# Batch 0 of an FFT filter ahead of an MLP: real and imaginary spectrum rows side by side, frequencies k1 and k1 + 12 on the two partition halves

## The chip, the core and the metric

The kernel runs on one core of a Trainium2 chip. The metric is the device time of one launch in microseconds. An engine's name stands for its instruction stream: PE is TensorE (PEld its weight loads), DVE is VectorE, ACT is ScalarE, POOL is GpSimd, SP is SyncE. POOL and SP also issue DMAs.

## What is computed

The input x has 8 batches of 3008 positions and 256 channels. Along the positions each channel is filtered in the frequency domain, with a complex filter for each frequency and channel; then every position goes through a two-layer MLP with an exact GELU, 256 to 2048 to 256.

```python
X = np.fft.rfft(x, axis=1)                      # x: (8, 3008, 256)
Y = X * (filt_r + 1j * filt_i)[None, :, :]      # filters: (1505, 256)
y = np.fft.irfft(Y, n=3008, axis=1)
h = y.reshape(24064, 256) @ w_in                # (256, 2048)
g = 0.5 * h * (1.0 + erf(h / np.sqrt(2.0)))
out = g @ w_out                                 # (2048, 256)
```

## The kernel before

**The transform.** 3008 is 47 x 64 (NA, NB), and the transform is done in two steps by matmuls with tables of sines: over the 47 (first index k1, of which 24 are needed, K1) and over the 64. Batch 0 has a path of its own, whose stages are c1, c1t, c2, c3, c3t and c4; it is the only work until its end, apart from tables and loads. Batches 1 to 7 go through s1, s2, s3, s4, in small pieces put between the matmuls of the MLP.

**Batch 0, stage by stage.** `c1` multiplies x by the 47-point table T1c and evicts into y_sb. `c1t(q)` transposes four k1 at a time into b_sb, with an eviction by ACT (the first by DVE and ACT together). `c2(p)` multiplies two k1 (2p and 2p + 1) by the table T2 into one PSUM bank: real and imaginary rows of one k1 lie on 128 partitions, and the two k1 stand side by side. DVE then multiplies that bank by the filter tile F, once by the real and once by the imaginary part of the filter (the tile p, 128 x 1024). `c3(p)` multiplies the result back with T3, and with T3i, a copy of T3 with real and imaginary rows exchanged and signs turned; the results go to vt_sb. `c3t` and `c4` transpose and do the inverse 47-point step into the ring y_sb, which the MLP reads.

**The filters.** F has 128 partitions. Rows 0 to 63 take the filter from HBM (32 rows directly, 32 in mirrored order), and rows 64 to 127 are a copy of rows 0 to 63, made by `dup_filters`: the first four k1 by DVE, the other twenty by POOL. `load_filters` is called for 4, 8 and 12 k1, and makes four DMAs each time. `move_filters` (SP) takes the filters from F to Fu, the form that batches 1 to 7 use.

**Tables T3 and T3i.** `table_3(q)` transposes eight k1 of T2 into a PSUM bank and `table_3_copy` evicts them. T3i is made from T3 by DVE for the first eight k1 (`table_3_turn`), and by ACT from PSUM for the others.

**Order.** Each engine works through its instructions in the order in which the program issues them, and waits for semaphores where data or buffers are wanted. The order is written out by hand at the end of the program; `warm_up(n)` puts n matmuls without use into TensorE's stream. DMAs that POOL issues go round eight semaphores, so the ninth waits until the first has landed. PSUM has two banks for c2 (tag w), one for the warm-ups, and five for the rest (tag n). POOL's order after x and the filters: w_in, the ten copies, small tables, then x of batch 1 (twelve DMAs into the tile that batch 0's x lay in), then w_out.

**The MLP.** `mm1` (L639) makes 512 tokens x 128 hidden units in two matmuls, ACT evicts with GELU (L642). `mm2_first` (L655) is the second layer of the first tiles; `mm2_seven` (L713) that of the others, with seven products in place of eight. A slot is one mm1 with what is put to it. `fold` (L109, L110) is the first step for batches 1 to 7, and reads x of that batch.

Of the kernel before, what the change touches and what calls it, by code (L numbers as in the profile page):

```python
# [31 lines left out]
class _Mix:  # L32
    def __init__(self, ctx, tc, x, filt_r, filt_i, w_in, w_out, out):
# [27 lines left out]
        self.F = c.tile([128, 2, K1, 256], BF16, name="F")  # L61
# [4 lines left out]
        self.T4a = f[0:96, 4096:7168].rearrange("p (w m) -> p w m", w=HB)  # L66
# [16 lines left out]
    def load_x(self, lo=0, n=32, hs=(0, 1)):  # L83
        nc = self.nc
        if lo == 0 and 0 in hs:
            xt = self.px.tile([128, HB, 256], BF16, tag="x", name="x_sb")
            self.st[0, "x"], self.st["x1"] = xt[0:2 * NA], xt.rearrange("p (h w) c -> p h w c", h=2)
        xt, o = self.st[0, "x"], NA
        xv = self.x[0].rearrange("(n1 h w) d -> h n1 w d", h=2, w=HB)
        for w in range(lo, lo + n, 8):  # L90
            for h in hs:
                nc.gpsimd.dma_start(out=xt[h * o:h * o + NA, w:w + 8, :], in_=xv[h][:, w:w + 8, :])
# [19 lines left out]
    def load_filters(self, k0, k):  # L112

        nc, D = self.nc, self.D
        for t, src in enumerate((self.filt_r, self.filt_i)):
            direct = _dram(src, k0 * D, [[NA * D, 32], [D, k], [1, D]])
            mirror = _dram(src, (NA - k0) * D, [[NA * D, 32], [-D, k], [1, D]])
            for q, a in enumerate((direct, mirror)):
                nc.gpsimd.dma_start(out=self.F[32 * q:32 * q + 32, t, k0:k0 + k, :], in_=a)

    def move_filters(self, m0, m):

        for c in (3, 2, 1, 0):
            for q in range(2):
                for e in range(2):
                    o, k = 32 * c + 16 * q, 6 * c + m0
                    for t in ((0, 1),) if c or m0 == 0 else ((0,), (1,)):
                        t = slice(t[0], t[-1] + 1)
                        i = self.F[32 * q + e:32 * q + 32:2, t, k:k + m, :]
                        self.nc.sync.dma_start(  # L130
                            out=self.Fu[o:o + 16, t, e ^ q, m0:m0 + m, :].rearrange("p t m c -> p t (m c)"),
                            in_=i.rearrange("p t m c -> p t (m c)"))

    def dup_filters(self, eng, k0, k):
        for k in range(k0, k0 + k, 2):
            o, i = (self.F[r:r + 64, :, k:k + 2, :].rearrange("p t a b -> p t (a b)") for r in (64, 0))
            (eng.copy if eng is self.nc.scalar else eng.tensor_copy)(out=o, in_=i)  # L137
# [69 lines left out]
    def table_2_angle(self, g, h):  # L207
# [4 lines left out]
        w = self.gen  # L212
        if h == 0:
# [3 lines left out]
            n6, self.n12 = col("n6"), col("n12")  # L217
            ts(out=n6, in0=self.n2, scalar1=6.0, scalar2=None, op0=ALU.mult)
            ts(out=self.n12, in0=self.n2, scalar1=12.0, scalar2=None, op0=ALU.mult)
            v.scalar_tensor_tensor(out=w[:, 0:6], in0=self.kk.unsqueeze(2).to_broadcast([128, 6, NB]), scalar=self.n2,  # L220
# [5 lines left out]
            ts(out=w[:, 6:12], in0=w[:, 0:6], scalar1=n6, scalar2=None, op0=ALU.add)  # L226
        else:
            ts(out=w[:, 12:24], in0=w[:, 0:12], scalar1=self.n12, scalar2=None, op0=ALU.add)
        k = slice(12 * h, 12 * h + 12)
        ts(out=self.gen_s.bitcast(I32), in0=w[:, k].bitcast(I32), scalar1=15, scalar2=None,  # L230
# [39 lines left out]
    def table_2_sin(self, h):  # L270
        k = slice(12 * h, 12 * h + 12)
        self.nc.scalar.activation(out=self.T2[:, k, 0, :], in_=self.gen_s.bitcast(I32), func=AF.Sin,
                                  scale=2.0 * PI / 2.0 ** 32)

    def table_2_swap(self, h):
        t2 = self.T2[:, 12 * h:12 * h + 12]
        for i in range(2):
            ps = self.bank("ps_sw", "n")
            self.nc.tensor.matmul(ps[:, 0:384], lhsT=self.swap, rhs=t2[:, :, 0, 32 * i:32 * i + 32],
                                  start=True, stop=True)  # L280
            self._evac(t2[:, :, 1, 32 * i:32 * i + 32], ps[:, 0:384].rearrange("p (k j) -> p k j", k=12),
# [10 lines left out]
    def table_3(self, q):  # L292

        self.t3 = ps = self.bank("ps_t3", "n", BF16)
        for i in range(8):
            self.nc.tensor.transpose(ps[:, 128 * i:128 * i + 128],
                                     self.T2[:, 8 * q + i].rearrange("p a b -> p (a b)"), self.eye)

    def table_3_copy(self, q, turn):

        k, v = slice(8 * q, 8 * q + 8), self.t3.rearrange("p (k n r) -> p k r n", k=8, r=2)
        if turn < 2:
            self._evac(self.T3[:, k], v, "act")
        if turn:
            for r in range(2):
                self._evac(self.T3i[:, k, r, :], v[:, :, 1 - r, :], "act", self.turn[r])

    def table_3_turn(self, q):

        k = slice(8 * q, 8 * q + 8)  # L310
        for r in range(2):
            self.nc.vector.tensor_scalar(out=self.T3i[:, k, r, :], in0=self.T3[:, k, 1 - r, :],
                                         scalar1=self.turn[r], scalar2=None, op0=ALU.mult)
# [37 lines left out]
    def table_u_rows(self, g):  # L351

        self.u0 = g.tile([128, 2, HB], BF16, name="u0")
        self.nc.gpsimd.tensor_copy(out=self.u0, in_=self.T3[:, 0, :, 0:HB])

    def table_u_pick(self, g):
# [3 lines left out]
        self.pick = g.tile([128, 2, 128], BF16, name="pick")  # L360
        p64 = g.tile([128, 1], FP32, name="p64")
        v.tensor_scalar(out=p64, in0=self.p, scalar1=-64.0, scalar2=None, op0=ALU.add)
        for t, p in enumerate((self.p, p64)):
            v.tensor_scalar(out=self.pick[:, t], in0=to, scalar1=p, scalar2=None, op0=ALU.is_equal)

    def table_u(self):
        ps = self.bank("ps_u", "f")
        for t in range(2):
            self.nc.tensor.matmul(ps[:, 64 * t:64 * t + 64], lhsT=self.pick[:, t],
                                  rhs=self.u0.rearrange("p r w -> p (r w)"), start=True, stop=True)  # L370
# [169 lines left out]
    def c1t(self, q, eng):  # L540
# [4 lines left out]
        b = self.st[0, "b", q]  # L545
        ps = self.bank("ps_c1t", "n", BF16)
        for i in range(8):
            self.nc.tensor.transpose(ps[:, 128 * i:128 * i + 128],
                                     self.at[:, i % 2, 4 * q + i // 2].rearrange("c h n r -> c (h n r)"), self.eye)
        n = 1024 // len(eng)  # L550
        for i, e in enumerate(eng):
            self._evac(b.rearrange("p a b -> p (a b)")[:, n * i:n * i + n], ps[:, n * i:n * i + n], e)

    def c2(self, p):

        nc = self.nc
        if p % 2 == 0:
            self.st[0, "w"] = self.pp.tile([128, 2, 4, 256], BF16, tag="p12", name="p12")
        w = self.st[0, "w"][:, :, p % 2 * 2:p % 2 * 2 + 2].rearrange("p t a c -> p t (a c)")
        self.st[0, "p", p] = w  # L560
        ps = self.bank("ps_c2", "w")
        for i in range(2):
            k = 2 * p + i
            nc.tensor.matmul(ps[:, 256 * i:256 * i + 256], lhsT=self.T2[:, k].rearrange("p a b -> p (a b)"),
                             rhs=self.st[0, "b", k // 4][:, k % 4, :], start=True, stop=True)
        f = self.F[:, :, 2 * p:2 * p + 2, :]
        if p < 11:
            nc.vector.tensor_tensor(out=w, in0=ps.unsqueeze(1).to_broadcast([128, 2, 512]),
                                    in1=f.rearrange("p t a b -> p t (a b)"), op=ALU.mult)
            return  # L570
        w, ps = w.rearrange("p t (a b) -> p t a b", a=2), ps.rearrange("p (a b) -> p a b", a=2)
        for c in (slice(0, 128), slice(128, 256)):
            nc.vector.tensor_tensor(out=w[:, :, :, c], in0=ps[:, :, c].unsqueeze(1).to_broadcast([128, 2, 2, 128]),
# [463 lines left out]
```

## Time and profile before

| | us |
|---|---|
| median of 3 runs (lowest, highest) | 735.17 (734.92, 736.33) |
| the profiled execution | 735.36 |
| its span, first to last instruction | 733.3 |
| first MLP matmul (L639) begins | 38.05 |
| filter products of batch 0 (L568, L573) | 16.01 to 30.43 |
| first and second half of w_out land | 44.73, 48.13 |

A row of the profile's list of groups names line, engine, operation, output and inputs, count, busy time and the mean duration of one. A row of a timeline begins with start and length in us; neighbours of the same kind are merged and counted. In brackets stands the idle time of the engine before the row, and what ended it. The busy time of PE counts matmuls that overlap once. The durations of matmuls include the way through the array; in a stream, a matmul of 512 columns takes 0.217 us and one of 128 columns 0.055 us.

### The profile page before, as it was taken

What the parts mean: (1) busy time and instruction counts of PE and PEld (TensorE: products, weight loads), DVE (VectorE), ACT (ScalarE), POOL (GpSimd) and SP (SyncE); (2) the same over time, 40 slices, a digit from 0 to 9 for tenths busy, and PEclk for the clock granted to TensorE, in tenths of its full rate; (3) what the DMA queues carried; (4) which work ended last, traced back from release to release, by engine and by line L of the source; (5) the groups of instructions that cost most, each with busy time, mean ns of one, the idle gap of its engine ahead of it and who ended that gap; (6) DMA issues with size and microseconds to landing.
All of it is one profiled execution on the core that took longest, in us unless ns stands there. A gap on an engine that the chain in (4) does not pass through costs nothing.

```text
span 733.3 us, 22221 instructions
## 1 busy us (share of the span) xinstructions
PE 723.4 (99%) x9165; PEld 505.7 (69%) x9165; DVE 598.6 (82%) x1091; ACT 575.3 (78%) x1049; POOL 288.4 (39%) x547
## 2 busy tenths in 40 slices
PE   7999999999999999999999999999999999999998
PEld 4856675676777666676777667666677767777776
DVE  8884698899878998788986999769988898675566
ACT  6997778688887888778887788877888788777773
POOL 7854377955223552134611364115531131122121
PEclk9999999999999999999999999999999999999999
DMA  9886634755355653545535455355544433411011
GB/s 148 162 178 151 166 85 111 217 120 104 86 157 150 127 103 104 163 126 126 127 105 172 109 124 130 93 152 142 114 106 128 148 107 94 114 40 49 30 59 59
DMA packets 81254, 87.72 MB, mean 120 GB/s; under 512 B 13393, under 2 KB 61137, under 8 KB 81153
## 3 DMA queue, kind: packets, MB, share of 16 engines
q0 software_dynamic: 22288, 39.50, 24.3%
q1 hardware_dynamic: 58449, 46.62, 23.5%
q8 instruction: 71, 1.16, 0.7%
q14 instruction: 30, 0.25, 0.1%
q10 hardware_dynamic: 416, 0.20, 0.1%
HBM read 54.00 MB, written 46.66 MB: 137 GB/s over the span
## 4 chain that ended last, share of the span: by engine, by line
PE 86%; DMA 4%; POOL 4%; DVE 3%; ACT 1%; issue 1%; SPq 0%; POOLq 0%; DVEq 0%
PE ps_h L639 41%; PE ps_o L713 35%; PE ps_s L514 3%; PE ps_o L655 3%; DMA x_sb<-in_x_dram 2%; PE ps_s L429 2%; PE ps_s L456 2%; PE ps_s L487 1%; DMA w_out_sb<-in_moe_w_out_dram 1%; DVE s_sb L684 1%; POOL F L137 1%; POOL x_sb L101 1%; DVE p L467 1%; DMA d_sb<-R 1%; ACT b_sb L325 1%
## 5 line engine op out<-in xcount | busy, mean ns | idle before, releaser
L642 ACT ACTIVATE g_sb<-ps_h 128x512 f16<-128x512 f32 x752 | 445.6, 602 | 138.3 <-PE ps_h L639 129.9
L639 PE MATMUL ps_h<-y_sb,w_in_sb 128*128 128x512 bf16 (+3 forms) x1600 | 445.4, 366 | 1.3 <-DVE p L467 0.7
L760 POOL DMA_DIRECT2D out_dram<-ost x231 | 131.3, 575 | 387.8 <-DVE ost L742 361.4
L713 PEld LDWEIGHTS <-g_sb 128*128 128x128 f16 x2816 | 184.5, 98 | 81.3 <-issue 14.6
L639 PEld LDWEIGHTS <-w_in_sb 128*128 128x128 bf16 x1600 | 126.4, 98 | 9.5 <-issue 2.8
L713 PE MATMUL ps_o<-w_sums,g_sb 128*128 128x128 f16 x1408 | 121.9, 219 | 0.4 <-DVE g_sb L690 0.2
L713 PE MATMUL ps_o<-w_sums,s_sb 128*128 128x128 f16 x1408 | 120.5, 219 | 0.0
L713 PEld LDWEIGHTS <-s_sb 128*128 128x128 f16 x1408 | 94.9, 98 | 36.4 <-issue 2.1
L684 DVE TENSOR_TENSOR s_sb<-g_sb 128x1024 f16<-128x1024 f16 x176 | 117.2, 697 | 0.4 <-ACT g_sb L642 0.3
L713 PE MATMUL ps_o<-w_out_sb,g_sb 128*128 128x128 f16 x1408 | 113.7, 219 | 0.0
L467 DVE TENSOR_TENSOR p<-ps_s,Fu 128x1024 bf16<-128x1024 f32 x84 | 101.6, 1218 | 9.1 <-PE ps_s L456 7.5
L101 POOL DMA_DIRECT2D x_sb<-in_x_dram x156 | 79.3, 515 | 3.6 <-DMA x_sb<-in_x_dram 1.8
L690 DVE TENSOR_TENSOR g_sb<-s_sb,g_sb 128x1024 f16<-128x1024 f16 x88 | 60.4, 687 | 1.5
L695 DVE TENSOR_TENSOR F<-g_sb 128x1024 f16<-128x1024 f16 x88 | 61.5, 698 | 0.0
L713 PE MATMUL ps_o<-w_out_sb,F 128*128 128x128 f16 x704 | 61.1, 219 | 0.0
L713 PEld LDWEIGHTS <-F 128*128 128x128 f16 x704 | 47.2, 98 | 15.5 <-issue 0.8
L735 DVE TENSOR_TENSOR t_sb<-t_sb,ps_o 128x256 f32<-128x256 f32 x44 | 18.4, 418 | 39.8 <-PE ps_o L713 39.3
L514 PEld LDWEIGHTS <-d_sb 96*128 96x128 bf16 x448 | 31.2, 97 | 26.5 <-issue 1.3
L325 ACT ACTIVATE y_sb<-ps_s 128x376 bf16<-128x376 f32 x95 | 45.5, 479 | 3.2 <-PE ps_s L514 3.2
L325 ACT ACTIVATE F<-ps_s 128x512 bf16<-128x512 f32 x83 | 45.5, 607 | 0.1
L327 DVE CAST a_sb<-ps_s 128x512 bf16<-128x512 f32 x54 | 34.7, 684 | 11.3 <-PE ps_s L429 11.1
L742 DVE TENSOR_TENSOR ost<-t_sb,ps_o 128x256 f32<-128x256 f32 x86 | 32.2, 416 | 13.6 <-PE ps_o L713 13.6
(159 smaller groups left out, 592.2 us busy)
## 6 DMA issues: line engine op xcount, KB each, us to landing
out_dram<-ost POOLq DMA_DIRECT2D x127, 128.0 KB, 3.0
b_sb<-R SPq DMA_DIRECT2D x21, 512.0 KB, 5.0
R<-F SPq DMA_DIRECT2D x84, 128.0 KB, 2.4
d_sb<-R SPq DMA_DIRECT2D x56, 192.0 KB, 4.2
R<-a_sb SPq DMA_DIRECT2D x108, 96.0 KB, 2.2
x_sb<-in_x_dram POOLq DMA_DIRECT2D x48, 94.0 KB, 2.7
x_sb<-in_x_dram POOLq DMA_DIRECT2D x48, 48.0 KB, 2.8
x_sb<-in_x_dram POOLq DMA_DIRECT2D x12, 188.0 KB, 5.1
```

What stands on the lines that cost most here:

```text
L101: self.nc.gpsimd.dma_start(out=xt[64 * v + to:64 * v + to + m, h, 4 * c:4 * c + 4 * n, :], in_=xv[h][at:at + m, w:w + 4 * n, :])
L325: self.nc.scalar.activation(out=out, in_=in_, func=AF.Copy, scale=1.0 if scale is None else scale)
L327: self.nc.vector.tensor_copy(out=out, in_=in_)
L467: v(out=w[:, a], in0=ps.unsqueeze(2).to_broadcast([128, 2, 2, 256]), in1=f.unsqueeze(1).to_broadcast([128, 2, 2, 256]), op=ALU.mult)
L514: nc.tensor.matmul(ps[:, 94 * i:94 * i + 94], lhsT=d[:, (grp % 2) * 4 + i, 128 * half:128 * half + 128], rhs=self.T4a[:, 4 * grp + i, 0:2 ...
L639: nc.tensor.matmul(ps[:, o:o + n], lhsT=w[:, dc], rhs=self.ring[:, dc, off:off + n], start=(dc == 0), stop=(dc == 1))
L642: nc.scalar.activation(out=self.st["g", t][:, jc, :], in_=ps, func=AF.Gelu)
L684: self.nc.vector.tensor_tensor(out=self.st["s", t][:, i:i + 2], in0=a, in1=b, op=ALU.subtract)
L690: self.nc.vector.tensor_tensor(out=a21[:, k], in0=self.st["s", t][:, k, 0], in1=a22[:, k], op=ALU.add)
L695: self.nc.vector.tensor_tensor(out=self.s4_sb[:, k], in0=a12[:, k], in1=s2[:, k], op=ALU.subtract)
L713: nc.tensor.matmul(ps[:, (m + 1) % 2, sub, :], lhsT=a[:, i, 128 * sub:128 * sub + 128], rhs=b[:, i], start=i == 0, stop=i == 7)
L760: eng.dma_start(out=out, in_=tile_[lo - r0:lo - r0 + n])
```

## The change

In c2, the rows of a bank are no longer real and imaginary parts of one k1: the bank's column halves hold the real and the imaginary part, and its partition halves hold k1 = p and k1 = p + 12. Each partition then has one frequency, so that F has 12 k1 in its free dimension, different ones on the two halves, and no row of F is a copy of another. The filter DMAs are now issued for 2, 4 and 6 k1 on each half, eight DMAs each time, 24 in all; `dup_filters` is gone. The matmuls of c2 have 64 output rows in place of 128, and those of c3 contract over 64 rows in place of 128, the two halves alternating. T3i comes from T3 by `tensor_scalar`: the first third on DVE as before, the second and third on POOL. `table_2_angle`, `table_2_sin` and `table_2_swap` work through T2 in another order of k1, with the same number of instructions. The two evictions of the first c1t read two PSUM banks in place of one.

POOL's order is now: x of batch 0 in ten DMAs instead of eight (the last two of 8 columns are halved), the 24 filter DMAs, the second third of T3i, w_in, half of batch 1's x, the last third of T3i, the other half, small tables, w_out. The table T4a gets a tile of its own; it lay in F before. table_u needs one matmul instead of two.

```diff
-        self.F = c.tile([128, 2, K1, 256], BF16, name="F")
+        self.F = c.tile([128, 2, K1 // 2, 256], BF16, name="F")
...
-        self.T4a = f[0:96, 4096:7168].rearrange("p (w m) -> p w m", w=HB)
+        self.T4a = c.tile([96, HB, 96], BF16, name="T4a")
...
     def load_filters(self, k0, k):
         for t, src in enumerate((self.filt_r, self.filt_i)):
-            direct = _dram(src, k0 * D, [[NA * D, 32], [D, k], [1, D]])
-            mirror = _dram(src, (NA - k0) * D, [[NA * D, 32], [-D, k], [1, D]])
-            for q, a in enumerate((direct, mirror)):
-                nc.gpsimd.dma_start(out=self.F[32 * q:32 * q + 32, t, k0:k0 + k, :], in_=a)
+            for h in range(2):
+                o, i = 64 * h, H * h + k0
+                nc.gpsimd.dma_start(out=self.F[o:o + 32, t, k0:k0 + k, :].rearrange("p k c -> p (k c)"),
+                                    in_=_dram(src, i * D, [[NA * D, 32], [1, k * D]]))
+                nc.gpsimd.dma_start(out=self.F[o + 32:o + 64, t, k0:k0 + k, :],
+                                    in_=_dram(src, (NA - i) * D, [[NA * D, 32], [-D, k], [1, D]]))
...
-    def dup_filters(self, eng, k0, k):
-        for k in range(k0, k0 + k, 2):
-            o, i = (self.F[r:r + 64, :, k:k + 2, :].rearrange("p t a b -> p t (a b)") for r in (64, 0))
-            (eng.copy if eng is self.nc.scalar else eng.tensor_copy)(out=o, in_=i)
...
     def table_3(self, q):
         for i in range(8):
-            self.nc.tensor.transpose(ps[:, 128 * i:128 * i + 128],
-                                     self.T2[:, 8 * q + i].rearrange("p a b -> p (a b)"), self.eye)
+            for h in range(2):
+                self.nc.tensor.transpose(ps[64 * h:64 * h + 64, 128 * i:128 * i + 128],
+                                         self.T2[:, K1 // 2 * h + 4 * q + i // 2, i % 2, :], self.eye)
...
+    def table_3_turn(self, q, eng):
+        t, u = (x[:, 4 * q:4 * q + 4].rearrange("p k q r n -> p (k q) r n") for x in (self.T3, self.T3i))
         for r in range(2):
-            self.nc.vector.tensor_scalar(out=self.T3i[:, k, r, :], in0=self.T3[:, k, 1 - r, :],
-                                         scalar1=self.turn[r], scalar2=None, op0=ALU.mult)
+            eng.tensor_scalar(out=u[:, :, r, :], in0=t[:, :, 1 - r, :], scalar1=self.turn[r], scalar2=None, op0=ALU.mult)
...
     def c1t(self, q, eng):
+        n = 8 // len(eng)
+        for j, e in enumerate(eng):
+            ps = self.bank("ps_c1t", "n", BF16)
+            for i in range(n * j, n * j + n):
+                k = 2 * q + i // 4 + K1 // 2 * (i // 2 % 2)
...
     def c2(self, p):
-        for i in range(2):
-            k = 2 * p + i
-            nc.tensor.matmul(ps[:, 256 * i:256 * i + 256], lhsT=self.T2[:, k].rearrange("p a b -> p (a b)"),
-                             rhs=self.st[0, "b", k // 4][:, k % 4, :], start=True, stop=True)
+        for r in range(2):
+            for h in range(2):
+                nc.tensor.matmul(ps[64 * h:64 * h + 64, 256 * r:256 * r + 256], lhsT=self.T2[:, K1 // 2 * h + p, r, :],
+                                 rhs=self.st[0, "b", p // 2][:, p % 2 * 2 + h, :], start=True, stop=True)
...
+            v(out=w[:, :, :, c], in0=ps[:, :, c].unsqueeze(1).to_broadcast([128, 2, 2, n]),
+              in1=self.F[:, :, p, c].unsqueeze(2).to_broadcast([128, 2, 2, n]), op=ALU.mult)
...
     def c3(self, p, np=2):
         for i in range(np):
             w = self.st[0, "p", p + i]
-            for half in range(2):
-                for k in range(2):
-                    for t in range(2):
-                        c, o = 128 * (2 * i + k), 256 * k + 128 * half
-                        t3 = (self.T3i if t else self.T3)[:, 2 * (p + i) + k]
-                        self.nc.tensor.matmul(ps[half][:, c:c + 128], lhsT=w[:, t, o:o + 128],
-                                              rhs=t3.rearrange("p a b -> p (a b)"), start=t == 0, stop=t == 1)
+            for f in range(2):
+                for j in range(4):
+                    for h in range(2):
+                        t, r, o, d = j // 2, j % 2, 128 * (np * f + i), slice(64 * h, 64 * h + 64)
+                        t3 = (self.T3i if t else self.T3)[d, p + i, r]
+                        self.nc.tensor.matmul(ps[h][:, o:o + 128], lhsT=w[d, t, r, 128 * f:128 * f + 128],
+                                              rhs=t3.rearrange("p a b -> p (a b)"), start=j == 0, stop=j == 3)
...
-    m.load_x(16, 16)
+    m.load_x(16, 8)
+    m.load_x(24, 4)
+    m.load_x(28, 4)
...
-    for k, n in ((0, 4), (4, 8), (12, 12)):
+    for k, n in ((0, 2), (2, 4), (6, 6)):
         m.load_filters(k, n)
-    m.load_w_in()
...
     m.table_3(1)
-    m.dup_filters(nc.vector, 0, 4)
     m.warm_up(1)
     m.c1t(0, (False, act))
-    m.dup_filters(nc.gpsimd, 4, 20)
     m.move_filters(0, 2)
     m.c1t(1, (act,))
-    m.table_3_copy(1, 0)
+    m.table_3_copy(1)
+    m.table_3_turn(1, nc.gpsimd)
+    m.load_w_in()
+    for h in range(2):
+        m.load_x_pairs(1, 0, h, 2)
     m.c2(0)
...
-    m.table_3_copy(1, 2)
...
-            if q != 3:
-                m.warm_up(2)
+            if q == 2:
+                m.table_3(2)
+                m.table_3_copy(2)
+                m.table_3_turn(2, nc.gpsimd)
+                for h in range(2):
+                    m.load_x_pairs(1, 2, h, 2)
+            m.warm_up(1 if q == 2 else 2)
             m.c2(2 * q + 1)
         if q < 6:
             m.c3(2 * q - 2)
-            if q == 3:
-                m.table_3(2)
-                m.table_3_copy(2, 1)
-            else:
-                m.warm_up(1)
+            m.warm_up(1)
...
-    for c in (0, 2):
-        for h in range(2):
-            m.load_x_pairs(1, c, h, 2)
```

## The prediction

> **What bounds the kernel now.** I read the page first, then the table of stretches, the timelines of DVE, PE and POOL in the first 45 us, the waits, and the sources of single lines. From the page:
>
> ```profile
> PE 723.4 (99%) x9165; PEld 505.7 (69%) x9165; DVE 598.6 (82%) x1091; ACT 575.3 (78%) x1049; POOL 288.4 (39%) x547
> PE   7999999999999999999999999999999999999998
> ```
>
> TensorE is full everywhere but in the first of 40 slices (18.3 us), and the change touches only what comes before and just after that. So what counts is when the MLP's first matmul (L639, at 38.05 us) can start, and what PE loses just behind it. Each us of delay there is a us at the end. The table of stretches (width, then busy us and instructions per engine):
>
> ```profile
> core 0: us, PE busy (x) PEld busy (x) DVE busy (x) ACT busy (x) POOL busy (x), PEclk, DMA share, GB/s
> 10.00:20.00 10.00, 9.10 (x110) 6.27 (x107) 7.74 (x14) 8.45 (x15) 7.53 (x14) 1.00 1.15 172
> 20.00:30.00 10.00, 9.52 (x122) 7.92 (x123) 10.00 (x11) 9.61 (x17) 9.75 (x16) 1.00 0.74 154
> 40.00:50.00 10.00, 9.39 (x73) 4.26 (x73) 8.98 (x15) 9.61 (x20) 3.35 (x8) 1.00 1.04 206
> ```
>
> From 20 to 30 us DVE is the only engine without a gap, but PE has only half a us to spare. The DVE timeline names the work (start, length, line, count):
>
> ```profile
> 14.29 0.80 DVE L137 COPY F<-F 64x1024 bf16<-64x1024 bf16 x2
> 16.01 2.35 DVE L568 TENSOR_TENSOR p<-ps_c,F 128x1024 bf16<-128x1024 f32 x2 [0.47 <-PE ps_c L564]
> 18.96 10.27 DVE L568 TENSOR_TENSOR p<-ps_c,F 128x1024 bf16<-128x1024 f32 x9 [0.59 <-POOL F L137]
> 29.15 1.28 DVE L573 TENSOR_TENSOR p<-ps_c,F 128x512 bf16<-128x512 f32 x2
> ```
>
> These are the filter products of c2, 1.14 us each (10.27/9); the last ends at 30.43, and the transposes c3t start 0.97 later. The wait of 0.59 is for the POOL copies of the filters, which waited for the filters' DMAs. POOL's timeline, whose issue times matter most here:
>
> ```profile
> 6.47 1.11 POOL L119 DMA_DIRECT2D F<-in_filt_r_dram  x2
> 12.66 0.58 POOL L119 DMA_DIRECT2D F<-in_filt_i_dram  x1 [0.47 <-DMA x_sb<-in_x_dram]
> 13.24 1.11 POOL L119 DMA_DIRECT2D F<-in_filt_r_dram  x2
> 17.90 9.99 POOL L137 COPY F<-F 64x1024 bf16<-64x1024 bf16 x10 [1.21 <-DMA F<-in_filt_i_dram]
> 29.02 4.63 POOL L101 DMA_DIRECT2D x_sb<-in_x_dram  x9
> ```
>
> A filter DMA costs POOL 0.5 to 0.6 us to issue, whatever its size. Between 7.96 and 12.66 each starts 0.93 behind the one before: eight DMAs may be under way, and the ninth waits for the first to land, which 188 KB pieces of x do every 0.93 us.
>
> **What goes.** Twelve filter copies: two on DVE (0.80 us) and ten on POOL (9.99 us). Four ACT evictions that turned T3 into T3i, 0.57 us apart, 2.3 us. ACT's relief is worth nothing by itself, since DVE and PE end later than ACT in this stage. Without the DVE copies, and with a PSUM bank for each half, the first b_sb eviction can begin behind four transposes, about 14.75 instead of 15.12. c2(0) on PE follows at 15.3 and its product at 15.7 (before: 15.60 and 16.01, so 0.41 between them): 0.3 us sooner, if the filters are there.
>
> **Filters: 24 issues for 12, same bytes.** In POOL's order the two extra x pieces take the two issues up to 7.5. Four filters start as before, at 7.96, 8.90, 9.83 and 10.77. The next four wait for x pieces of half the size, so POOL's own 0.54 per issue is the limit, and the eighth starts at 12.9. The remaining sixteen at 0.54 end at 22.1; the sixteenth DMA starts at 17.2, the twenty-fourth at 21.6. Time to landing lies between 2.2 us (the fastest x load later on, L101) and 5.4 (the median of L119 now, with queues full). I take L101's median, 2.8, since small DMAs issued this slowly leave the queues partly empty. So the first group (k1 offsets 0 and 1, wanted by c2(0)) lands at 15.7, just in time; the second (c2(2)) at 20.0, against 18.96 now; the third (c2(6)) at 24.4. Even without later waits, DVE would end c2 at 24.6 + 5 x 1.14 + 1.28 = 31.6, 1.1 later than now.
>
> A rule speaks against this part: the Trainium skill, "DMA: Bandwidth & Descriptors", "Rules for kernel authors", calls two transfers to disjoint partition halves not worth it and wants one wide transfer. The same page's fit in "Anatomy of one DMA — SWDGE (gpsimd) path", about 2.0 us plus bytes at 436 GB/s, makes an estimate of 2.1 us to land; by it the filters come 0.7 sooner and the sum would be 736.7, but L101's 2.2 is the trace's fastest and 2.8 its median, so the row stands.
>
> **PE: same columns, other tile shapes.** c2 makes four products of 64 output rows for two of 128, in pairs on the two column halves; c3 makes 32 of 64 rows deep for 16 of 128, in pairs on the two row halves; table_3 likewise. Side by side, streaming takes as long as now (c2 0.22, c3 0.89). The trace has such tiles in s2:
>
> ```profile
> 58.84 0.59 PE L639 MATMUL ps_h<-y_sb,w_in_sb 128*128 128x512 bf16 x2
> 59.36 0.63 PE L456 MATMUL ps_s<-b_sb,T2p 64*32 64x256 bf16 x32
> 59.93 0.50 PE L655 MATMUL ps_o<-w_out_sb,g_sb 128*128 128x256 f16 x3
> ```
>
> Two of 512 columns normally take 0.43 (L639 repeats at that pace), so s2 should start at 59.27 and starts 0.09 later. Its 32 products in eight tiles are four rounds of 0.11, and the next line starts 0.13 behind them. So tiles do run side by side, and each change of shape costs about 0.1 us (bounds 0, if a wait hides it, and 0.13). From c2(4) to c2(11) the new order has 19 such changes: 1.9 us. Now that stretch runs from 20.24 to 28.16 on PE, with 7.27 us of work: seven c2 1.54, two c1t 0.88, table_3 0.44, three c3 2.67, eight warm-ups of 0.217. After, it has ten warm-ups: 7.70 + 1.9 = 9.6. c2(4) needs the PSUM bank that the product of c2(2) frees, 20.0 + 1.14, so 21.25; then c2(10) starts at 30.0, its product at 30.4, and the last product runs from 31.55 to 32.83: 2.4 later than 30.43.
>
> Weights are where the shapes could cost more. c3 now loads 16 blocks and takes 0.89, so a load and its 128 columns take at most 0.056. The Trainium skill, "TensorE: Matmul & The Clock Gate", "LDWEIGHTS (loading the stationary operand)", says that load time goes with the columns and not with the rows, so half-height blocks save nothing. The row bounds c3 between 0.89 (pairs overlap) and 32 x 0.056 = 1.78; s2's 32 loads within 0.56 us are nearer to overlap, so I take 0.89. If the rule is combined with no overlap, the sum is the third rival's.
>
> **T3i on POOL.** Four tensor_scalar of 512 columns replace the ACT work. A POOL copy of 1024 columns takes 1.04 (L137), an undisturbed tensor_scalar of 128 columns 0.61:
>
> ```profile
> L364 POOL TENSOR_SCALAR pick<-cols,p x2: 607/1075/1543, 51.7 to 53.2; 128x128 bf16<-128x128 f32 x2
> ```
>
> So one costs from 0.6 (copy rate) to 1.8 (0.2 fixed, the rest in proportion); I take 1.0, nearer the copy, which is bf16 as well. Behind the filters: memset and turn(1) end at 24.3, w_in (2 x 0.55) at 25.4, the first six x DMAs at 28.5, turn(2) at 30.5. c3(4) wants turn(1) at 26.3, c3(8) wants turn(2) at 31.2. Both fit, by 0.7 us only in the second case.
>
> **What moves.** w_in is issued at 24.3 instead of 15.4 and takes up to 10.9 to land (L155): 35, ahead of the first L639. Half of batch 1's x is issued at 25.4 instead of 29.0, the other half at 30.5. w_out follows at 35.5 (now 37.17). The filters for later batches (SP, L130) wait for the third group and have until 59.8. The one PE wait that this removes:
>
> ```profile
> PE ps_o L655 <- DMA w_out_sb<-in_moe_w_out_dram: 0.3, 1, 0.3
> ```
>
> ACT, 9.61 of 10 busy from 40 to 50, leaves little else to win there; fold and s1 shift with the rest. T4a as its own tile, and the smaller table_u, lie under a full PE: nothing.
>
> **Sum.** +2.4 for c2, +0.1 for c3(11) entering its shape, -0.3 for w_out: +2.2. The profiled execution took 735.36 (span 733.3), 0.19 above the median of 735.17; from the median, 737.4. This kernel's measurement tells 0.2%, about 1.5 us, from no change.
>
> **Rivals.**
> 1. Faster. Filters land as soon as now and DVE hides the shape changes: the products run without a gap from 15.7, 11 x 1.14 + 1.28, to 29.5 (-0.9), and x and w_out take all 0.61 us of PE's gaps in 40 to 50: 733.6. For it: POOL loses 10 us of copies. It decides if the second group lands by 18, that is if issues take under 0.42; no DMA row of POOL is under 0.49. Chance 0.15.
> 2. About no change. Landing takes 2.2, shape changes half: c2 ends at 31.0, +0.6 - 0.3: 735.5. Chance 0.22.
> 3. Slower by more, through weight loads that do not overlap: 0.89 on three c3 before c2(11) and about 1.8 on those behind it: 741.8. Chance 0.12.
> 4. Slower by more, through POOL: at 1.8 each, turn(2) ends at 33.7, c3(8) waits 2.5 for it: 740.0. Chance 0.13.
> The claims themselves are half true: filters are read once, but in twice as many DMAs, and x comes sooner by one half only.
>
> **Numbers.** The forecast holds 0.38. Faster is the first rival, no change the second, the rest is slower: 0.15, 0.22, 0.63. The range from 733.6 to 742.0 runs from the first to the third; POOL at still slower rates, or both slow rivals together, lie outside.
>
> **What would show it.** Right: F issues on POOL without a break to about 22; a DVE wait for filter DMAs ahead of the third product, near 20; PE gaps of 0.1 at each change between L553, L571 and full tiles; last product near 32.8; L639 starting near 40.4. Wrong: the third product before 18.5, c3 at 1.5 us or more (rival 3), a PE wait at L571 for POOL (rival 4), or L639 at 38 or sooner.

## The result, and the profile after

The changed kernel takes 739.77 us (median; 739.39 to 740.25) where the kernel before took 735.04 in the same series: a ratio of 1.0061, 95% interval 1.0043 to 1.0078. That is 4.7 us slower, on the forecast's side and inside its range, but twice the forecast of 2.2. The profiled execution took 740.25, with a span of 738.5.

From the page of the changed kernel, the lines that answer to the two of before:

```profile
PE 718.2 (97%) x9161; PEld 504.9 (68%) x9310; DVE 598.4 (81%) x1089; ACT 574.5 (78%) x1045; POOL 292.5 (40%) x553
PE   7999999999999999999999999999999999999998
```

The shape is the same: PE full in all but the first slice, so the loss is again in what happens before the MLP's first matmul and just behind it. (The 97% against 99% of before are not idle time: 144 of the 1600 matmuls of L626 have no record in this trace, while all their weight loads have.) That matmul (now L626) starts at 42.88 instead of 38.05, 4.83 later. Between the first c3t and that matmul lie 6.65 us in both kernels, so the whole of it has arisen by c3t (36.23 against 31.40).

The DVE timeline of the changed kernel shows the filter products (L558; start, length):

```profile
17.05 2.36 DVE L558 TENSOR_TENSOR p<-ps_c,F 128x1024 bf16<-128x1024 f32 x2 [1.41 <-DMA F<-in_filt_r_dram]
20.82 4.74 DVE L558 TENSOR_TENSOR p<-ps_c,F 128x1024 bf16<-128x1024 f32 x4 [1.42 <-DMA F<-in_filt_i_dram]
26.21 2.36 DVE L558 TENSOR_TENSOR p<-ps_c,F 128x1024 bf16<-128x1024 f32 x2 [0.64 <-PE ps_c L553]
28.98 2.36 DVE L558 TENSOR_TENSOR p<-ps_c,F 128x1024 bf16<-128x1024 f32 x2 [0.42 <-PE ps_c L553]
31.52 2.42 DVE L558 TENSOR_TENSOR p<-ps_c,F 128x1024 bf16<-128x1024 f32 x3 [0.18 <-PE ps_c L553]
```

Before, DVE ran without a gap from 18.96 to 30.43. Now it waits twice for filter DMAs, and from the seventh product on it waits for PE (the seventh may also have waited for the third filter group, landed at 25.93): the bound has moved. PE's timeline from c2(4) on (L553 is c2, L571 c3, L311 the warm-ups):

```profile
22.11 0.41 PE L553 MATMUL ps_c<-b_sb,T 128*64 128x256 bf16 x4 [0.72 <-DVE p L558]
...
31.41 0.39 PE L311 MATMUL ps_warm<-ones 128*128 128x512 bf16 x1
31.95 0.41 PE L553 MATMUL ps_c<-b_sb,T 128*64 128x256 bf16 x4
32.29 0.29 PE L571 MATMUL ps_c<-T,p 64*128 64x128 bf16 x4
32.88 0.96 PE L571 MATMUL ps_c<-T,p 64*128 64x128 bf16 x28 [0.30 <-POOL T L305]
33.77 0.39 PE L311 MATMUL ps_warm<-ones 128*128 128x512 bf16 x1
34.09 0.62 PE L571 MATMUL ps_c<-T,p 64*128 64x128 bf16 x16
...
36.23 1.50 PE L588 MATMUL ps_c3t<-eye,vt_sb 128*128 128x128 bf16 x24 [0.32 <-PE ps_c L571]
```

The same points in the kernel before (L564 is c2, L586 c3, L601 c3t):

```profile
20.24 0.39 PE L564 MATMUL ps_c<-b_sb,T 128*128 128x256 bf16 x2 [0.33 <-DVE p L568]
...
28.16 0.38 PE L564 MATMUL ps_c<-b_sb,T 128*128 128x256 bf16 x2
...
30.14 0.74 PE L586 MATMUL ps_c<-T,p 128*128 128x128 bf16 x8
...
31.40 1.50 PE L601 MATMUL ps_c3t<-eye,vt_sb 128*128 128x128 bf16 x24
```

Three points of PE's order divide the 4.83 us: the start of c2(4), the start of c2(11) and the start of c3t.

| | before | after | more |
|---|---|---|---|
| c2(4) starts | 20.24 | 22.11 | 1.87 |
| from there to c2(11) | 7.92 | 9.84 | 1.92 |
| from there to c3t | 3.24 | 4.28 | 1.04 |

The experiments below take these three rows apart. In each the same three numbers are read from PE's timeline. Since PE's order is fixed between them, the second and third repeat to 0.02 us where nothing else comes in. The start of c2(4) does not: in the four traces with the same 24 filter DMAs (the changed kernel, e1, e3, e4) it lies at 22.11, 21.49, 22.46 and 21.53, so the first row is known to about half a us only.

The chain of work that ended last, in order of time (start, length), shows that POOL is as late as PE:

```profile
21.72 0.56 POOL F L121
...
25.47 0.62 POOL w_in_sb L152
...
26.64 3.04 POOL x_sb L102 x6
29.68 0.00 issue
29.68 3.16 POOL T L305 x2
32.84 0.04 issue
32.88 0.96 PE ps_c L571 x28
```

It runs from the filter issues through w_in, batch 1's x and the last third of T3i to c3(8).

Two smaller differences lie under the full PE, later on. Counted from the first GELU to the 25th, the changed kernel takes 0.2 us more than the runs that give table_u 128 rows again (below); between the 25th and the 61st, 0.45 more than before. The second is a wait on ACT (its timeline; L317 evicts s3 into v_sb, a part of F):

```profile
75.50 0.59 ACT L317 ACTIVATE F<-ps_s 128x512 bf16<-128x512 f32 x1
76.66 0.60 ACT L317 ACTIVATE F<-ps_s 128x512 bf16<-128x512 f32 x1 [0.56 <-DMA out_dram<-ost]
```

### The profile page after: what moved, and what is told of

It reads as the page before. It is cut to its first block, busy times and chain, and to the rows that moved or that the text cites. A ratio compares the mean times of both kernels' runs of the same rounds, so it can differ in the third digit from the quotient of the medians.

```text
span 738.5 us, 22359 instructions
## 1 busy us (share of the span) xinstructions
PE 718.2 (97%) x9161; PEld 504.9 (68%) x9310; DVE 598.4 (81%) x1089; ACT 574.5 (78%) x1045; POOL 292.5 (40%) x553
## 4 chain that ended last, share of the span: by engine, by line
PE 83%; POOL 5%; DMA 3%; DVE 3%; ACT 2%; issue 2%; SPq 1%; DVEq 0%; POOLq 0%
PE ps_o L700 37%; PE ps_h L626 35%; PE ps_s L502 3%; PE ps_s L417 2%; PE ps_o L642 1%; PE ps_s L444 1%; PE ps_s L475 1%; ACT g_sb L629 1%; SPq L132 1%; DMA x_sb<-in_x_dram 1%; DVE s_sb L671 1%; DMA b_sb<-R 1%; ACT y_sb L317 1%; POOL F L121 1%; POOL x_sb L102 1%
## 5 line engine op out<-in xcount | busy, mean ns | idle before, releaser
L626 PE MATMUL ps_h<-y_sb,w_in_sb 128*128 128x512 bf16 (+3 forms) x1456 | 414.7, 365 | 2.0 <-DVE p L455 0.8
L626 PEld LDWEIGHTS <-w_in_sb 128*128 128x128 bf16 x1600 | 126.4, 98 | 9.7 <-issue 2.9
L317 ACT ACTIVATE y_sb<-ps_s 128x376 bf16<-128x376 f32 x95 | 45.5, 479 | 3.1 <-PE ps_s L502 3.1
L317 ACT ACTIVATE F<-ps_s 128x512 bf16<-128x512 f32 x83 | 45.7, 609 | 0.7 <-DMA out_dram<-ost 0.6
```

The costliest lines, as they stand in the source:

```text
L317: self.nc.scalar.activation(out=out, in_=in_, func=AF.Copy, scale=1.0 if scale is None else scale)
L626: nc.tensor.matmul(ps[:, o:o + n], lhsT=w[:, dc], rhs=self.ring[:, dc, off:off + n], start=(dc == 0), stop=(dc == 1))
```

## The experiments

All times stand beside runs of the kernel before on the same chip; its medians there were 735.06 (first four runs), 734.68 (next four) and 735.23 (last two).

**T3i's last two thirds on DVE** (e1_turn_dve).

```diff
-    m.table_3_turn(1, nc.gpsimd)
...
     m.c2(1)
+    m.table_3_turn(1, nc.vector)
...
-                m.table_3_turn(2, nc.gpsimd)
...
             m.c2(2 * q + 1)
+            if q == 2:
+                m.table_3_turn(2, nc.vector)
```

> The changed kernel, with the second and third part of T3i made on DVE (in its gaps behind c2(1) and c2(5)) instead of POOL. Theory A (POOL's queue is the last link: filters, then T3i, whose last part ends at 32.8 us, and c3(8) waits for it): the wait at c3(8) goes, and the time falls by about 1.0 us, to 738.8; batch 1's x is issued some 6 us sooner and gains nothing. Theory B (the shape changes on TensorE are the main cost): c3(8) starts where PE's own order lets it, at most 0.5 sooner, to 739.3 or no change. Theory C (the late landing of the filters alone): no change, 739.8.

Measured: 739.79 us, ratio 1.0059 (1.0047 to 1.0071). The wait at c3(8) is gone in the trace, with c3(8) and c3(9) in one piece behind c2(11):

```profile
31.41 0.41 PE L553 MATMUL ps_c<-b_sb,T 128*64 128x256 bf16 x4
31.76 1.07 PE L571 MATMUL ps_c<-T,p 64*128 64x128 bf16 x32
```

The row from c2(11) to c3t falls from 4.28 to 3.80. So POOL's lateness is worth 0.48 us, and what remains there is PE's own: theory B's size, not theory A's. On DVE the four operations take 0.34 to 0.36 us each. The median did not fall, though the profiled execution, at 739.28, is the fastest of its five: half a us is at the edge of what the times tell, and here only the trace tells it.

**Filters in two groups, 16 DMAs** (e2_16dma).

```diff
-    for k, n in ((0, 2), (2, 4), (6, 6)):
+    for k, n in ((0, 4), (4, 8)):
```

> The changed kernel, with the filters loaded in two groups (4 and 8 offsets of k1) instead of three: 16 DMAs for the same bytes. Theory A: POOL's issues end 4.3 us sooner and T3i's last part at 28.5; the first filter product starts later (17.5 instead of 17.05) but there is no second wait; the time falls by 1.0 to 1.3 us, to 738.6. Theory B: filters are not the limit, the products move by 0.3 at most: 739.5. Theory C: the products run without a gap from 17.5, last one ended by 31.3 instead of 33.9, and the time falls by 2.5, to 737.3.

Measured: 739.19 us, ratio 1.0053 (1.0041 to 1.0065), 0.6 below the changed kernel. c2(4) starts at 21.60; the wait for the second group has moved to the fifth product (23.34, until a landing at 23.16). T3i is ready at 28.9, and again 3.80 lie between c2(11) and c3t, with 9.84 between c2(4) and c2(11). The time lies between theories A and B; theory C, products without a gap, is out. The start of c2(4) is within what the runs with 24 DMAs show, so what the trace shows for certain is that POOL's wait is gone.

**v_sb's second tile at another offset of F** (e3_vsb). F is half as large now, and v_sb's second tile came to lie where the last filter moves (move_filters) still read. The edit puts it in a part that is read sooner.

```diff
-        self.v_sb = [f[:, o:o + 1024].rearrange("p (c d) -> p c d", c=2) for o in (2048, 3072)]
+        self.v_sb = [f[:, o:o + 1024].rearrange("p (c d) -> p c d", c=2) for o in (2048, 5120)]
```

> The changed kernel, with the second of the two eviction tiles of s3 (v_sb, which lie in F) moved within F, to a place whose filters are moved to Fu early. Theory: of the time lost behind the start of the MLP, 0.5 us arises near 76 us, where ACT's last eviction of s3 waits for the last filter move out of the smaller F; without it 739.3. Rival: that eviction is late for another reason (the output DMA that the list of waits names): 739.8.

Measured: 739.41 us, ratio 1.0055 (1.0042 to 1.0067). ACT's timeline has both evictions together, without the wait:

```profile
75.37 1.08 ACT L317 ACTIVATE F<-ps_s 128x512 bf16<-128x512 f32 x2
```

The way from the 25th to the 61st GELU is 33.88 us, as in the kernel before, against 34.33 in the changed one: 0.45 us. The profile had named an output DMA as the releaser; the edit shows that the place in F decided, and in the changed kernel the last filter move landed at 76.40, just ahead of the eviction.

**No warm-ups in the c2 stage** (e4_nowarm): the 18 `warm_up` matmuls from c2(0) to c3(11) are left out.

> The changed kernel without the 18 warm-up matmuls between c1t(0) and c3(11): 3.9 us less of matmuls on PE, and about 15 shape changes fewer. Theory A: nothing, since c3(8) still waits for POOL until 32.8 and the rest follows from there: 739.8, or 0.3 less for what stands behind it. Theory B: c2(11) and c3 come up to 2 us sooner: 737.8. If TensorE needs the warm-ups to keep its pace, matmuls of 512 columns get longer than 0.217 and the time rises.

Measured: 740.24 us, ratio 1.0065 (1.0052 to 1.0078): nothing gained, although 3.9 us of PE work are gone. PE then waits for filters and DVE, and this is what follows (PE's timeline, then two lines of the table of stretches, whose last three columns are granted clock, DMA share and GB/s):

```profile
28.01 0.41 PE L553 MATMUL ps_c<-b_sb,T 128*64 128x256 bf16 x4 [1.50 <-DVE p L558]
29.14 0.41 PE L553 MATMUL ps_c<-b_sb,T 128*64 128x256 bf16 x4 [0.72 <-DVE p L558]
29.48 1.71 PE L571 MATMUL ps_c<-T,p 64*128 64x128 bf16 x32
```

```profile
26.31:29.72 3.41, 1.19 (x26) 0.72 (x22) 2.99 (x3) 1.19 (x3) 3.41 (x8) 1.00 0.93 163
29.72:33.13 3.41, 3.36 (x54) 2.58 (x50) 2.96 (x4) 1.08 (x2) 3.26 (x3) 0.50 1.07 219
```

After 3.41 us in which PE was busy for 1.19, the granted clock is 0.50 for the next 3.41, and a c3 that takes 1.07 elsewhere takes 1.71. In the traces of the kernels with warm-ups the clock stays at 1.00 here. So in this kernel the warm-ups keep the clock, and the experiment can't tell what their share of PE's order costs.

**The kernel before with c2 in halves** (e5_before_half): only the tile shape of c2 is that of the change.

```diff
-            nc.tensor.matmul(ps[:, 256 * i:256 * i + 256], lhsT=self.T2[:, k].rearrange("p a b -> p (a b)"),
-                             rhs=self.st[0, "b", k // 4][:, k % 4, :], start=True, stop=True)
+            for r in range(2):
+                nc.tensor.matmul(ps[64 * r:64 * r + 64, 256 * i:256 * i + 256], lhsT=self.T2[:, k, r, :],
+                                 rhs=self.st[0, "b", k // 4][:, k % 4, :], start=True, stop=True)
```

> The kernel before, with one thing changed: each c2 matmul of 128 output rows is made as two of 64 rows on the two column halves, so that c2 has the changed kernel's tile shape and nothing else of it. Theory A (each change of tile shape costs PE 0.10 us): 15 more changes between c2(4) and c2(11), 1.5 us on a stretch with 0.65 us of gaps, so c2(11) starts at about 29.0 instead of 28.16, c3t at about 32.4 instead of 31.40, and the time is 1.0 us longer, 736.1. Theory B (the changes lie beside waits for DVE): the products stay without a gap to 30.4, and the time is the same within 0.2 us.

Measured: 735.97 us, ratio 1.0013 (1.0004 to 1.0021). Its table of stretches, from c2(4) to c2(11):

```profile
20.18:29.04 8.86, 8.86 (x110) 5.46 (x109) 8.15 (x8) 8.40 (x14) 8.58 (x15) 1.00 0.70 151
```

c2(11) starts at 29.04 and c3t at 32.29 (expected 29.0 and 32.4). PE has no gap any more, and 8.86 less the 7.27 us of work in that stretch is 1.59. Counted in PE's timeline, the shape changes 14 times there (not 15, as the expectation has it), so 0.114 each; in the changed kernel, 9.84 less 7.70 of work over 19 changes gives 0.113. Theory B falls: the change costs PE, and PE's time is the end's.

**Four edits together** (e6_mended): e1, e2 and e3, and table_u's matmul on 128 rows (the upper 64 zeros).

> The changed kernel with four edits together: T3i's second and third part by DVE, filters in two groups (16 DMAs), v_sb's second tile at an offset of F that move_filters reads early, and table_u's matmul with 128 rows (64 of them zeros). Theory A (the terms add): 0.6 for the filters, 0.35 to 0.45 for v_sb, 0.2 for table_u, and up to 0.6 for the POOL wait, so 738.0 to 738.6. Theory B (PE's own order sets c3t at 35.2, so T3i gives nothing more): 738.6, c3t at 35.2.

Measured: 738.40 us, ratio 1.0047 (1.0035 to 1.0060); c3t at 34.97. The two rows of PE's order are 9.84 and 3.80 once more, the first with PE busy for 9.84, so without any wait. From the first GELU to the 25th it takes 19.03 instead of 19.24, as in every run with table_u's matmul on 128 rows (e7, e8, e10), while e1 to e4 and e9 have 19.24. PE's timeline around that matmul (L357), in the changed kernel and then here:

```profile
60.40 0.59 PE L626 MATMUL ps_h<-y_sb,w_in_sb 128*128 128x512 bf16 x2
60.93 0.23 PE L357 MATMUL ps_u<-u,pick 64*128 64x128 bf16 x1
61.09 0.50 PE L642 MATMUL ps_o<-w_out_sb,g_sb 128*128 128x256 f16 x3
```

```profile
59.15 0.59 PE L626 MATMUL ps_h<-y_sb,w_in_sb 128*128 128x512 bf16 x2
59.58 0.22 PE L357 MATMUL ps_u<-u,pick 128*128 128x128 bf16 x1
59.64 0.49 PE L642 MATMUL ps_o<-w_out_sb,g_sb 128*128 128x256 f16 x3
```

The three steps take 0.69 us from start to start with 64 rows and 0.49 with 128: 0.20 for two changes of shape. The time is in theory A's range; the 3.80, with T3i early, says with theory B that PE's own order sets c3t. Both named nearly the same time, so the run separates them only by the rows.

**Warm-ups in the shape of c2** (e7_warm_split): e6, with each warm-up of the c2 stage as two of 64 output rows.

```diff
+        if split:
+            for i in range(2 * n):
+                o = i % 2 * 64
+                self.nc.tensor.matmul(ps[o:o + 64], lhsT=self.ones[:, 0:64], rhs=self.ones, start=True, stop=True)
+            return
```

> The run before (e6) with the warm-up matmuls of the c2 stage made as two of 64 output rows on the two column halves, like c2, so that they take as long but stand in c2's tile shape. Between c2(4) and c2(11) 10 changes of shape remain of 19. Theory A (PE's shape changes set the end of c2): 0.5 to 0.9 us sooner than e6, c3t at 34.3 to 34.7. Theory B (filters and DVE set it): the same as e6 within 0.2 us.

Measured: 738.82 us, ratio 1.0055 (1.0041 to 1.0068): by the times, no different from e6. The trace differs. From c2(4) to c2(11) it takes 9.17 instead of 9.84 for the same columns:

```profile
21.74:30.91 9.17, 9.09 (x178) 6.47 (x175) 8.41 (x10) 6.89 (x11) 3.51 (x7) 1.00 1.10 218
```

That is 0.67 for nine changes fewer, but with a wait in it: c2(9) starts 0.70 behind the warm-ups ahead of it (27.95 to 28.65) where e10, with the same order, has 0.42. e10's stretch has no wait (8.91 from start to start):

```profile
20.64:29.54 8.90, 8.90 (x176) 6.48 (x178) 8.25 (x8) 6.66 (x11) 8.24 (x13) 1.00 0.97 178
```

So nine changes fewer are worth 0.93 us, 0.10 each. In e7 the first filters landed 0.5 later (first product at 17.55 against 17.06), and c2(4) came 0.41 later, so c3t comes at 34.74, only 0.23 sooner. The median says nothing for theory A; the stretch does.

**A shorter tail** (e8_tail): e7 without the two warm-ups between c3(8), c3(10) and c3(11).

> e7 without the warm-ups between c3(8), c3(10) and c3(11), which takes away two matmuls of 0.22 us and four changes of shape behind c2(11). Theory A (PE's order sets the tail behind the last product): 0.85 us sooner than e7 at most, 0.5 where c3(11) then waits for the last product; the tail from the last product to c3t falls from 1.8 to about 1.2. Theory B (the last product sets it, with evictions behind): within 0.2 us of e7.

Measured: 738.69 us, ratio 1.0047 (1.0034 to 1.0060). From c2(11) to c3t it takes 3.41 instead of 3.83, and c3t follows 1.13 behind the end of the last product (33.40), close to the 1.2 that theory A expected. But the stretch from c2(4) to c2(11) took 9.69 here instead of 9.17, with waits for DVE in it, whose fifth product waited for filters until 23.66; so c3t comes only 0.21 sooner (34.53), and the median shows no difference. Another reason why e7 and e8 don't fall below e6 stands far behind the edits, in this line of e8's PE timeline:

```profile
464.20 0.33 PE L507 MATMUL ps_s<-T4a,d_sb 96*128 96x94 bf16 x4 [0.80 <-DMA d_sb<-R]
```

From the 61st GELU to the end e6 takes 641.01 us, e7 641.67 and e8 641.99. Single waits so far behind the edits differ from execution to execution, and by up to 1 us they hide what an edit gains ahead of the MLP.

**Half as many filter DMAs for the same bytes** (e9_12dma). To fill 64 partitions each, the DMAs read equally spaced rows and not the rows that the transform needs: this version leaves out the mirrored order.

```diff
+                if h == 0:
+                    nc.gpsimd.dma_start(out=self.F[o:o + 64, t, k0:k0 + k, :].rearrange("p k c -> p (k c)"),
+                                        in_=_dram(src, i * D, [[23 * D, 64], [1, k * D]]))
+                else:
+                    nc.gpsimd.dma_start(out=self.F[o:o + 64, t, k0:k0 + k, :],
+                                        in_=_dram(src, (NA - i) * D, [[23 * D, 64], [-D, k], [1, D]]))
```

> The changed kernel with half as many filter DMAs, 12, each to 64 partitions, for the same bytes. To do so it reads other rows of the filters, equally spaced ones on 64 partitions instead of 32 direct and 32 mirrored ones; this leaves out the mirrored order, and only its times count. Theory A (24 issues on POOL are what makes the filters late): issues end near 15, no wait for F behind the first product, the third product at about 18.5 instead of 20.8, T3i's turns on POOL end by about 25, so the POOL wait at c3(8) goes too; c2(4) starts near 20.4, and with 9.7 to c2(11) and 3.8 behind it c3t starts at 33.9 to 34.3, about 2 us sooner: 737.5 to 738.0. Theory B (bytes and queues set the landing): landings as before, third product at 20 or later, and less than 0.7 us sooner: 739.1 or more.

Measured: 738.22 us, ratio 1.0035 (1.0023 to 1.0047), 1.55 below the changed kernel by the medians (1.74, when each is counted from the kernel before beside it). The DVE timeline:

```profile
16.16 2.36 DVE L560 TENSOR_TENSOR p<-ps_c,F 128x1024 bf16<-128x1024 f32 x2 [0.59 <-PE ps_c L555]
19.14 3.49 DVE L560 TENSOR_TENSOR p<-ps_c,F 128x1024 bf16<-128x1024 f32 x3 [0.62 <-PE ps_warm L313]
```

The first product no longer waits for filters. The third still does: it starts 0.18 behind the landing of its group's last DMA (18.96), just as in the changed kernel (20.64 and 20.82), though the view names a warm-up as the releaser. So even with 12 DMAs and no copies the third product comes no sooner than in the kernel before (18.96). What holds c2(4) here is PE:

```profile
15.71:20.68 4.97, 4.82 (x71) 2.77 (x71) 3.90 (x4) 4.23 (x6) 3.60 (x4) 1.00 1.10 166
```

From c2(0) to c2(4) PE works without a wait (the 0.15 that the line lacks is a warm-up without a record): 3.95 us of matmuls and nine changes of shape, 0.113 each. c2(4) starts at 20.68, 0.44 behind the kernel before, 0.11 of it at c2(0) already and 0.33 from there. The rows behind it are 9.84 and 3.80, so c3t at 34.32, at the end of what theory A gave; the median is 0.2 above its range. The issues end at 16.4 instead of 22.3. So the first row falls from 1.87 to 0.44 (c2(4) comes 0.8 to 1.8 sooner than in the four traces with 24 DMAs), and the 0.48 of POOL in the third goes: both come from the number of filter DMAs, if the rows read here cost the same as the right ones, which no run shows.

**All of it** (e10_all_12dma): e9 with e3's offset, table_u on 128 rows, and the warm-ups of e8.

> The run before (e9, with the same filter rows) with v_sb's tile, table_u, the split warm-ups and the shorter tail of the runs above. If the parts add: c2(4) near 20.4, 9.2 us to c2(11), 3.4 behind it, so c3t at 33.0, 1.6 behind the kernel before, and with w_out's wait gone the time is 736.0 to 736.6. If the products' chain on DVE takes over from PE, c3t stays at 33.5 or later and the time at 737.

Measured: 736.41 us, ratio 1.0014 (1.0005 to 1.0022), within what was expected if the parts add, with c3t at 32.96: c2(4) at 20.64, then 8.91 and 3.41. Here c2(4) does wait for the third product, which starts at 19.36, 0.18 behind the landing of its filters (19.18). Against the kernel before, 0.40, 0.99 and 0.17 us are left, 1.56 together; less the 0.28 of w_out below that is 1.28, and the medians differ by 1.18. So even with half the DMAs none of these versions is faster than the kernel before.

## Why the prediction was right in sign and short in size

**Where it is decided.** Right: of the 5.16 us by which the last instruction comes later, 4.83 lie ahead of the MLP's first matmul and pass to the end undiminished.

**Filter issues.** Right: F issues on POOL without a break until 22.28 (forecast 22.1), and a DVE wait for filters ahead of the third product, at 20.82 (forecast "near 20"). *Issue and landing were mis-sized.* For landing the forecast took 2.8 us, the median of a later x load. The sources of the two lines give medians of 3.1 (L119) and 3.3 (L121, below):

```profile
DMA to landing us min/median/max: 2.1/3.3/4.2
```

The groups landed at 16.88, 20.64 and 25.93 instead of 15.7, 20.0 and 24.4, and c2(4) came at 22.11 instead of 21.25: 0.86 us. Of these, 0.32 are the issue (the sixteenth DMA began at 17.52, not 17.2), 0.32 its landing (3.12, not 2.8), and 0.18 lie between landing and product, where the forecast had nothing; in e1, e3 and e4, with the same DMAs, the difference from the forecast is 0.24 to 1.21. The fit cited from the Trainium skill, "DMA: Bandwidth & Descriptors" ("Anatomy of one DMA — SWDGE (gpsimd) path"), gave 2.1 us, which is the fastest of L121's twelve. The same page's rule against two transfers to disjoint partition halves ("Rules for kernel authors") gives as its reason that both share the same DMA engines. e9, with transfers of 64 partitions for two of 32, agrees with the advice, by 1.55 us of the medians; what its trace shows as the reason is POOL's issues, which end at 16.4 instead of 22.3.

**Changes of tile shape.** Right in mechanism and nearly in size: 0.1 us each was taken from one step into s2, and e5 gives 0.114. The stretch from c2(4) to c2(11) was forecast at 9.6 and is 9.84, here and in e2, e3, e6 and e9. The forecast counted changes only from c2(4) on; e9 shows that the nine ahead of it hold c2(4) at 20.68 even where it doesn't wait for filters. The Trainium skill, "TensorEngine Tiling (Array Packing)", "Key Properties", says that a change of tiling mode drains TensorE, without a price; 0.10 to 0.11 us is the price in these runs.

**Weight loads.** Right: c3's 32 half-height blocks take 1.07 us of busy time, as 16 full ones took 1.05. The third rival is out.

**The tail behind the last product: the step that failed most.** The forecast kept the 0.97 us of the kernel before between the last product and c3t, and added 0.1. It is 2.29 (33.94 to 36.23), 1.22 more. In the kernel before, PE was ahead and waited there for DVE's last product, so the 0.97 was the little that came behind DVE. Once PE is late, all that it does behind c2(11) counts. e1, e2, e3, e6 and e9 give 3.80 from c2(11) to c3t in place of 3.24: 0.56, with six changes of shape in it. The changed kernel's 4.28 has POOL's 0.48 on top. The prediction had worked out when c2(10) starts on PE, but not followed PE's order to c3t.

**T3i on POOL.** Mis-sized within its bounds: 1.6 us each, not 1.0.

```profile
L305 POOL TENSOR_SCALAR T<-T,turn_r x2: 1600/1606/1612, 22.4 to 29.7; 128x512 bf16<-128x512 bf16 x2
L305 DVE TENSOR_SCALAR T<-T,turn_r x1: 339/339/339, 13.2 to 13.2; 128x512 bf16<-128x512 bf16 x1
```

The upper bound, from the 128-column row of the same operation, was the better neighbour than the copy of the same type. The last third ended at 32.82 instead of 30.5, and c3(8) lost 0.48 us: the fourth rival, at a fifth of its price, since c3(8) itself came later too. Its sign, a PE wait at L571 for POOL, stood in the forecast's list of signs of being wrong, and it came. That the measured 739.77 lies beside this rival's 740.0 is luck: 0.48 of its 2.5 us is there, and the rest of the loss has other causes.

**w_out.** Right by accident. The 0.28 us wait is gone, but not because w_out came sooner: it was issued at 40.6 (before: 37.2; forecast 35.5), since POOL stood still for 2.64 us ahead of the x issue at 36.96. The matmul that reads it came later still, at 49.1 instead of 44.8, and so finds it landed.

**"T4a and table_u lie under a full PE: nothing."** Wrong: table_u's one matmul of 64 rows changes the shape twice in a full PE and costs 0.20 (e6). And the smaller F brought the wait of ACT, 0.45 us net, which the prediction did not look for (e3).

**Sum.** Forecast 2.2, plus 0.86 (issue and landing), 0.24 (stretch), 1.22 (tail, with POOL's 0.48 in it), 0.20 (table_u) and 0.45 (v_sb) makes 5.17; the last instruction of the profiled execution comes 5.16 later than before. By the medians the loss is 4.73. The 0.4 between them is not traced to a step; the four runs of the changed kernel lie 0.86 apart themselves.

What stays open: why e1's gain in the trace doesn't show in its median, whether the mirrored order of the filter rows has a cost of its own, and what sets the start of c2(4) half a us sooner or later with the same DMAs.

## What to carry to other kernels

When a change makes another engine the bound, the slack measured behind the old bound is no longer a term of the sum: follow the new engine's order, instruction by instruction, to the point that sets the end. Where the releaser that a view names has no part in what waits, compare the start with the landings: in e3 and e9 it was another DMA. Packing two small matmuls side by side costs no columns, but each change of tile shape costs about 0.1 us in a full TensorE, for single small matmuls and warm-ups too; group equal shapes or give the filler the shape of its neighbours. Splitting a load so that no copy is needed pays only if the issuing engine has room for the issues: here 12 more of them made the filters later than the 12 copies had, and with as many DMAs as before (e9) the third product still came no sooner.

## What the runs showed of the hardware

- A POOL `tensor_scalar` of 128 x 512 bf16 with a per-partition scalar takes 1.60 us, 4.7 times the 0.34 of DVE, while a POOL copy of 1024 columns (64 partitions, bf16) in the kernel before took 1.04.
- A stretch that is only partly idle can bring the clock down: in e4, 3.41 us with PE busy for 1.19 and gaps of 1.50 and 0.72 were followed by 3.41 us at a granted clock of 0.50. A single gap of 1.60 in e7, ahead of 18.83, was not: the clock stayed at 1.00. The Trainium skill, "TensorE: Matmul & The Clock Gate", Part 1, names one idle window of about 3.4 us in its table of states; the two stretches of e4 have that length, but the first was not idle throughout.
- The time from issue to landing rose when the DMAs were larger and fewer: medians of 4.5 and 5.2 us for the two lines in e9, against 3.1 and 3.3; the filters as a whole still landed 3.1 us sooner (22.86 against 25.93).
